# Scores of an attention kernel as 64 by 64 products on four tiles of TensorE's array

## The chip, the cores and the metric

The kernel runs on one core of one Trainium2 chip. The metric is the device time of one execution in microseconds. A core has TensorE (matrix products; its loads of stationary weights are listed apart), VectorE, ScalarE, GpSimd and SyncE, and 16 DMA engines. TensorE holds a stationary operand in an array of 128 rows by 128 columns; a moving operand streams past it, column by column, and the products are summed in PSUM. The array can be addressed in parts: by row halves (an operand with 64 rows), by column halves (64 output rows), or by both.

## The reference, cut to what matters

`reference.py` computes, for 4 batches, 8 heads, 576 positions and head width 64, causal attention mixed with a memory term, and then a two-layer network:

```python
scores = scale * np.matmul(q, k.transpose(0, 1, 3, 2))
scores = np.where(causal, -1000000000.0, scores)
a = np.exp(scores - scores.max(-1, keepdims=True))
a /= a.sum(-1, keepdims=True) + 1e-09
local = np.matmul(a, v)
...
out = g * mem_out + (1 - g) * local
h = x @ w_in
g = np.maximum(h, 0.0) + np.log1p(np.exp(-np.abs(h)))
return g @ w_out
```

The input `x` of the network is `out` with its 8 heads side by side (2304 rows of 512), and the hidden width is 2048. All operands are fp32.

## The kernel before, in words

Heads are taken in pairs: `p` counts 4 pairs, and a pair's two heads of 64 channels fill the 128 partitions of a q or k tile (head 0 in partitions 0 to 63, head 1 in 64 to 127). Each pair of each batch is worked in two windows of query positions: window A holds chunks 0 and 1 (positions 0 to 255), window B holds chunks 2, 3 and 4 (256 to 575, the last chunk with 64 positions). That makes 32 halves (4 batches, 2 windows, 4 pairs).

For each half, in the names of the code: q and k are loaded (`qA`, `kA`, or `qB`, `kB`, L986 to L998); `memory` (L770) makes the memory term (`sm`, then `mA` or `mB`); `chunks` (L503) makes the scores (`s`, a PSUM tile of two banks, one for each head), their row maxima (`nm`, L548), the powers (`P`, L559) and the normalized weights, which are turned either by TensorE (`turned`, L668) or by a transposing DMA (`PTA` or `PTB` from `PHL`, L629); and `values` (L819) sums memory term and weighted values in `xp` (L825, L837, L852). When a block of positions has its four pairs, `fill` (L897) runs the first 7 of the network's 16 hidden blocks on it (L384) beside the attention of the next; `rest` (L920) does the others at the end (L384, L950). Weights are unpacked by `decode` (L466), partly with TensorE products (L488, L489).

The scores are made in `scores` (L521). For chunks 0 to 3 each head is one product call (L528): the stationary operand is 128 query positions of the head's 64 partitions, the moving operand the keys up to and including the chunk (128, 256, 384 or 512 columns), and the output is 128 partitions of the head's bank. An fp32 product call leaves two weight loads and two matmuls in the trace. The two heads lie on the two row halves of the array. Chunks 0 and 1 are made in one go (8 matmul records), chunks 2 and 3 each by itself (4 records). Chunk 4 takes both heads on the full array (L532). After the products of each go, the causal mask is added by products with an identity (L539 for window A, L543 for chunks 2 and 3, L534 for chunk 4), and VectorE waits for the last of these.

The order of every engine's work is fixed ahead by a planner (`Plan`, L95): it takes the operations with estimated durations and ranks (the tables at the head of the file), plays them through, and the instructions are issued in the order that comes out. In stretches where the planner sees TensorE idle it issues spare products (L1033). The scores are one operation of the planner with an estimate of its own (L576).

Of the kernel before, what the change touches and what calls it, by code (L numbers as in the profile page):

```python
# [272 lines left out]
def attn_softplus_moe(  # L273
# [15 lines left out]
    MM = nc.tensor.matmul  # L289
# [213 lines left out]
    def chunks(u, win, b, p, cs, ks):  # L503
# [5 lines left out]
        so = [0, 128] if both else [0] * len(cs)  # L509
# [11 lines left out]
        def scores(js):  # L521
            for j in js:
                c, n, sv, qv, kv = cs[j], ns[j], ss[j](), q()[:, 130:], kk()
                cq = c * 128 - q0
                if c < 4:
                    for h in range(2):
                        rr = slice(64 * h, 64 * h + 64)
                        MM(sv[:, h, so[j]:so[j] + n], lhsT=qv[rr, cq:cq + 128], rhs=kv[rr, :n], start=j == js[0],  # L528
                           stop=True, skip_group_check=True)
                else:  # L530
                    for i in range(2):
                        MM(sv[:, i, :288], lhsT=win.qz(), rhs=kv[:, 288 * i:288 * i + 288], start=True, stop=True)  # L532
            if m == 1:
                MM(sv[:, 1, 224:288], lhsT=identb, rhs=mask4, start=False, stop=True, skip_group_check=True)  # L534
                return
            for h in range(2):
                e = so[js[-1]] + ns[js[-1]]
                if len(js) == 2:
                    MM(sv[:, h, 0:512].rearrange("p (c n) -> p c n", c=2)[:, :, 0:128], lhsT=identb,  # L539
                       rhs=mask.unsqueeze(1).to_broadcast([128, 2, 128]), start=False, stop=True,  # L540
                       skip_group_check=True)
                else:
                    MM(sv[:, h, e - 128:e], lhsT=identb, rhs=mask, start=False, stop=True, skip_group_check=True)  # L543
# [22 lines left out]
        for j, c in enumerate(cs):  # L566
            k, s, nm, pt = ks[j], ss[j], nms[j], pts[j]
            if m == 1:
                win.qz = QZ[win.no // 2 % 2]
                op("POOL", 470, k + RK["qz"], lambda: P.tensor_tensor(  # L570
                    out=win.qz().rearrange("p (h q) -> p h q", h=2),
                    in0=q()[:, 130 + 256:130 + 320].unsqueeze(1).to_broadcast([128, 2, 64]),
                    in1=own.rearrange("p (h q) -> p h q", h=2), op=ALU.mult), r=[q], w=[win.qz])
            if not both or j == 0:
                js = range(len(cs)) if both else [j]
                op("PE", 1080 if both else (450, 660, 968, 1180, 1050)[c], k, lambda js=js: scores(js),  # L576
                   r=[q, kk] + ([win.qz] if m == 1 else []), mode="S" if m == 2 else "f",
                   w=[s] + ([(pt, "s")] if guard else []))
            op("DVE", 147 + 2.08 * ns[j] if m == 2 else 746, k, lambda j=j: maxima(j), r=[s], w=[(nm, j)])
# [23 lines left out]
        for j, c in enumerate(cs):  # L603
            k, pt, phl = ks[j], pts[j], phls[j]
            if c < 4:
                n, nk = ns[j], c + 1
# [367 lines left out]
    for hi_, (b, p, w) in enumerate(halves):  # L974
        u = units[b, p]
        cs, q0, n = WINS[w]
# [114 lines left out]
```

## Time and profile before

| what | us |
|---|---|
| three runs | 612.47, 614.54, 616.35 |
| their median | 614.54 |
| the profiled execution, its own time | 612.59 |
| its span, from the first to the last instruction | 610.8 |

All rows are from that one profiled execution. PE is TensorE's matmuls, PEld its weight loads, DVE is VectorE, ACT ScalarE, POOL GpSimd, SP SyncE; L528 is line 528 of the kernel. A matmul's record runs from its issue to its modelled end, so records that follow one another overlap, and a start may stand ahead of the end of the load that the matmul needs. A shape such as 64*128 is rows by columns of the array; 128*64 has 64 columns.

### The profile page before, as it was taken

To read this page: it belongs to the slowest core of one execution; us is meant where nothing else is said; L and a number is where in the kernel's file an instruction comes from. 1 tells how busy PE (TensorE), PEld (TensorE's weight loads), DVE (VectorE), ACT (ScalarE), POOL (GpSimd) and SP (SyncE) were. 2 spreads that over 40 slices of the span, in tenths; PEclk is the share of its full clock that TensorE was granted. 3 is DMA by queue.
4 is the path that set the end of the run, shared out by engine and by line. 5 is a ranking of instruction groups with operands and counts; after the bars stand their busy time and mean duration, and the time that the engine had idled before them with its cause. 6 is when DMAs were issued, how large, how long until landed. Compare 5 with 4: busy or idle time off the path is not lost.

```text
span 610.8 us, 12312 instructions
## 1 busy us (share of the span) xinstructions
PE 590.8 (97%) x4610; PEld 531.6 (87%) x4610; DVE 353.2 (58%) x805; ACT 302.6 (50%) x854; POOL 170.8 (28%) x262
## 2 busy tenths in 40 slices
PE   6998999999999999999999999999999999999996
PEld 5666769787887787978799999999999999999996
DVE  6778888787877798868982777651212121212121
ACT  5767866566766686668743443433222222222221
POOL 3455433435433434325532344330000000000000
PEclk9999999999999999999999999999999999999999
DMA  8634559958999799966976643333314140522011
GB/s 314 212 131 147 168 161 230 174 202 180 194 198 216 187 179 193 171 172 158 174 124 172 214 136 122 105 126 117 104 36 129 47 135 3 169 72 70 1 44 35
DMA packets 129243, 87.38 MB, mean 143 GB/s; under 512 B 86176, under 2 KB 120992, under 8 KB 129184
## 3 DMA queue, kind: packets, MB, share of 16 engines
q1 hardware_dynamic: 129184, 86.60, 55.4%
q8 instruction: 36, 0.59, 0.4%
q14 instruction: 23, 0.19, 0.1%
HBM read 47.88 MB, written 18.22 MB: 108 GB/s over the span
## 4 chain that ended last, share of the span: by engine, by line
PE 65%; DMA 2%; DVE 1%; SPq 0%; ACT 0%; POOL 0%; issue 0%; DVEq 0%; ACTq 0%
PE h L384 35%; PE s L950 21%; PE s L528 3%; PE xp L837 3%; PE s L532 1%; PE sm L799 1%; DMA PTA<-PHL 1%; PE xp L825 1%; DMA qA<-in_nat_dram 1%; DMA kA<-in_nat_dram 1%; PE s L543 1%; DVE PHL L620 0%; DVE vb L763 0%; PE s L539 0%; SPq L914 0%
## 5 line engine op out<-in xcount | busy, mean ns | idle before, releaser
L384 PE MATMUL h<-xhl,w 128*128 128x256 f32 (+1 forms) x1536 | 227.8, 298 | 0.0
L384 PEld LDWEIGHTS h<-xhl,w 128*128 128x128 f32 x1536 | 210.5, 189 | 1.6 <-issue 0.5
L317 DVE TENSOR_TENSOR g<-gl,g 128x256 fp32r<-128x256 f32 (+1 forms) x128 | 60.0, 472 | 161.9 <-ACT g L323 161.7
L887 ACT ACTIVATE gl<-h 128x256 f32<-128x256 f32 (+1 forms) x128 | 52.1, 409 | 179.3 <-PE h L384 176.9
L950 PE MATMUL s<-g,w 128*128 128x320 f32 (+1 forms) x948 | 139.3, 297 | 0.0
L950 PEld LDWEIGHTS s<-g,w 128*128 128x128 f32 x948 | 131.1, 188 | 0.0
L384 PE MATMUL h<-g,w 128*128 128x256 f32 (+1 forms) x588 | 87.1, 299 | 0.0
L616 POOL TENSOR_SCALAR PHL<-P,rr 128x384 f16<-128x384 f32 (+3 forms) x100 | 57.2, 588 | 80.1 <-DVE rr L596 22.2
L384 PEld LDWEIGHTS h<-g,w 128*128 128x128 f32 x588 | 78.7, 190 | 0.7
L559 ACT ACTIVATE P<-s,nm 128x256 f32<-128x256 f32 (+3 forms) x128 | 66.4, 525 | 5.2 <-DVE PHL L620 2.6
L548 DVE TENSOR_REDUCE nm<-s 128x2 f32<-128x768 f32 (+2 forms) x64 | 51.4, 818 | 12.8 <-PE s L543 7.2
L323 ACT CAST g<-gl 128x256 fp32r<-128x256 f32 (+1 forms) x128 | 55.1, 433 | 3.9
L620 DVE SCALAR_TENSOR_TENSOR PHL<-P,rr,PHL 128x384 f16<-128x384 f32 (+3 forms) x100 | 56.0, 594 | 0.8 <-POOL PHL L616 0.8
L317 POOL TENSOR_TENSOR w<-wu,w 128x512 fp32r<-128x512 f32 x23 | 30.5, 1328 | 28.8 <-ACT w L323 28.8
L353 POOL TENSOR_SCALAR wu<-wu 128x512 f32<-128x512 f32 x32 | 20.4, 641 | 45.0 <-DVE wu L349 40.3
L528 PE MATMUL s<-kB,qB 64*128 64x384 f32 (+1 forms) x128 | 32.7, 588 | 0.0
L837 PEld LDWEIGHTS <-vb 128*64 128x64 f16 x508 | 24.6, 110 | 8.2 <-issue 2.4
L791 POOL TENSOR_TENSOR ph<-ph,pe 128x320 f32<-128x320 f32 (+1 forms) x22 | 18.5, 843 | 31.5 <-ACT pe L783 21.0
L360 DVE SCALAR_TENSOR_TENSOR wu<-ws,wu 128x512 int32<-128x512 int32 x32 | 26.6, 832 | 0.9
L559 ACT ACTIVATION_READ_ACCUMULATOR P<-s,nm 128x1 f32 x128 | 25.5, 199 | 0.0
L323 ACT CAST w<-wu 128x512 fp32r<-128x512 f32 x29 | 17.9, 618 | 13.9 <-DVE wu L364 13.7
L554 ACT ACTIVATE nm<-nm 128x2 f32<-128x2 f32 (+2 forms) x64 | 12.9, 201 | 23.9 <-DVE nm L548 17.3
(123 smaller groups left out, 648.9 us busy)
## 6 DMA issues: line engine op xcount, KB each, us to landing
ws<-in_w_in_dram SPq DMA_DIRECT2D x16, 512.0 KB, 3.7
ws<-in_w_out_dram SPq DMA_DIRECT2D x16, 512.0 KB, 3.4
va<-in_nat_dram SPq DMA_DIRECT2D x16, 320.0 KB, 4.0
xd<-xhl SPq DMA_DIRECT2D x16, 320.0 KB, 3.1
kB<-in_nat_dram SPq DMA_DIRECT2D x16, 288.0 KB, 3.7
xd<-xhl SPq DMA_DIRECT2D x16, 256.0 KB, 3.0
xhl<-xd SPq DMA_DIRECT2D x8, 512.0 KB, 4.7
xhl<-xd SPq DMA_DIRECT2D x6, 640.0 KB, 5.0
```

The source lines that it names most:

```text
L317: eng.tensor_tensor(out=out, in0=in0, in1=in1, op=ALU.subtract)
L323: A.copy(out, in_)
L360: V.scalar_tensor_tensor(out=ti(), in0=si(1), scalar=-0x40000000, in1=ti(), op0=ALU.bitwise_and, op1=ALU.bitwise_or)
L384: MM(out, lhsT=l, rhs=r, start=start and i == 0, stop=stop and i == len(pairs) - 1)
L528: MM(sv[:, h, so[j]:so[j] + n], lhsT=qv[rr, cq:cq + 128], rhs=kv[rr, :n], start=j == js[0], stop=True, skip_group_check=True)
L548: V.tensor_reduce(out=nm()[:, 2 * j * both:2 * j * both + 2], in_=s()[:, :, so[j]:so[j] + n], op=ALU.max, axis=AX.X, negate=True)
L559: A.activation(out=pt()[:, po[j] + h * n:po[j] + h * n + n], in_=s()[:, h, so[j]:so[j] + n], func=AF.Softplus, scale=SCALE, bias=nm()[:, o ...
L616: P.tensor_scalar(out=o[:, :, 0, h, :], in0=src, scalar1=rs, scalar2=0.0, op0=ALU.mult, op1=ALU.add)
L620: V.scalar_tensor_tensor(out=o[:, :, 1, h, :], in0=src, scalar=rs, in1=o[:, :, 0, h, :], op0=ALU.mult, op1=ALU.subtract)
L837: MM(xp()[64 * h:64 * h + 64, lo:n], lhsT=vb()[:, vi, kc, 64 * h:64 * h + 64], rhs=ptw()[:, kc * 4 + t * 2 + h, lo:n], start=False, stop=( ...
L887: op("ACT", 170 + .833 * n, -1, lambda: A.activation(out=gl()[:, :n], in_=hp()[:, :n], func=AF.Softplus, scale=XSC), r=[hp], w=[gl])
L950: MM(bank(dm), lhsT=l, rhs=r, start=f == f0 and q == 0 and (not small or dm % 2 == 0), stop=f == NF - 1 and q == 2, skip_group_check=True)
```

## The change

Each of the calls of L528 becomes two, with 64 query positions each: `e` picks the first or the second 64 of the chunk, as columns of the stationary operand and as partitions of the output. The moving operand is the same for both. The calls for the four combinations of head and `e` follow one another, so a go of one chunk has four calls in place of two. The masks, chunk 4, the planner's operations, durations and ranks are not touched.

```diff
                 if c < 4:
                     for h in range(2):
                         rr = slice(64 * h, 64 * h + 64)
-                        MM(sv[:, h, so[j]:so[j] + n], lhsT=qv[rr, cq:cq + 128], rhs=kv[rr, :n], start=j == js[0],
-                           stop=True, skip_group_check=True)
+                        for e in range(0, 128, 64):
+                            MM(sv[e:e + 64, h, so[j]:so[j] + n], lhsT=qv[rr, cq + e:cq + e + 64], rhs=kv[rr, :n],
+                               start=j == js[0], stop=True, skip_group_check=True)
                 else:
```

## Rows read from the trace of the kernel before

**Rows 1.** The page: busy time of each engine, and the granted clock by slice.

```profile
PE 590.8 (97%) x4610; PEld 531.6 (87%) x4610; DVE 353.2 (58%) x805; ACT 302.6 (50%) x854; POOL 170.8 (28%) x262
...
PEclk9999999999999999999999999999999999999999
```

**Rows 2.** Waits of matmuls on other engines: us in total, times, longest.

```profile
PE sm L1033 <- DVE mA L812: 2.9, 2, 2.5
PE s L528 <- DMA kA<-in_nat_dram: 2.7, 2, 1.5
PE sm L1033 <- DVE mB L812: 2.2, 1, 2.2
...
PE xp L837 <- DMA PTA<-PHL: 1.2, 2, 0.8
```

**Rows 3.** Windows: length, each engine's busy time (count), clock, DMA share, GB/s.

```profile
120.00:201.70 81.70, 78.16 (x656) 65.64 (x655) 66.37 (x167) 54.21 (x171) 32.09 (x51) 1.00 0.93 197
201.70:256.90 55.20, 55.20 (x440) 45.83 (x441) 47.34 (x113) 39.23 (x117) 22.80 (x39) 1.00 0.92 182
...
264.30:310.50 46.20, 46.20 (x362) 37.23 (x364) 39.13 (x91) 35.43 (x108) 23.40 (x34) 1.00 0.74 154
310.50:610.80 300.30, 295.65 (x2266) 293.80 (x2262) 101.47 (x192) 91.05 (x213) 37.16 (x39) 1.00 0.32 98
```

**Rows 4.** Waits of weight loads, lines 543 and 539: us, times, longest.

```profile
PEld L543 <- issue: 20.8, 32, 0.8
PEld L539 <- issue: 5.3, 16, 0.3
```

**Rows 5.** Timeline, three groups of line 528: start, us covered, engine, line, names, shape, count.

```profile
20.07 0.52 PEld L528 LDWEIGHTS s<-kA,qA 64*128 64x128 f32 x8 [0.17 <-issue]
...
28.27 0.19 PEld L528 LDWEIGHTS s<-kB,qB 64*128 64x128 f32 x2 [0.21 <-ACT ph L789]
...
28.70 0.49 PE L528 MATMUL s<-kB,qB 64*128 64x384 f32 x2
...
29.12 0.10 PEld L543 LDWEIGHTS <-identb 128*128 128x128 bf16 x1 [0.54 <-issue]
...
36.50 0.30 PEld L528 LDWEIGHTS s<-kB,qB 64*128 64x128 f32 x4 [0.17 <-issue]
...
37.03 0.59 PE L528 MATMUL s<-kB,qB 64*128 64x512 f32 x2
```

**Rows 6.** Line 528 in window B: shortest, median and longest record in ns.

```profile
L528 PEld LDWEIGHTS s<-kB,qB x128: 182/184/187, 28.3 to 304.4; 64*128 64x128 f32 x128
L528 PE MATMUL s<-kB,qB x128: 482/588/694, 28.3 to 304.9; 64*128 64x384 f32 x64, 64*128 64x512 f32 x64
```

**Rows 7.** Timeline, line 852: column halves at 128 by 64 and 64 by 64.

```profile
37.77 0.20 PEld L852 LDWEIGHTS xp<-PTA,va 128*64 128x64 f32 x4
...
38.04 0.39 PE L852 MATMUL xp<-PTA,va 128*64 128x256 f32 x2
38.26 0.39 PE L852 MATMUL xp<-PTA,va 128*64 128x128 f32 x4
...
89.07 0.20 PEld L852 LDWEIGHTS xp<-PTB,va 64*64 64x64 f32 x4 [0.28 <-issue]
89.33 0.19 PEld L488 LDWEIGHTS h<-wu,ident 128*128 128x128 f32 x1
```

**Rows 8.** Timeline, line 528 where TensorE came out of a wait.

```profile
7.76 0.55 PEld L528 LDWEIGHTS s<-kA,qA 64*128 64x128 f32 x8 [1.72 <-DMA qA<-in_nat_dram]
...
264.27 0.18 PEld L528 LDWEIGHTS s<-kA,qA 64*128 64x128 f32 x1 [1.43 <-DMA qA<-in_nat_dram]
...
264.27 0.22 PEld L528 LDWEIGHTS s<-kA,qA 64*128 64x128 f32 x2 [1.43 <-DMA qA<-in_nat_dram]
```

**Rows 9.** Windows, line 528 alone: length, matmuls (count), loads (count), clock, DMA.

```profile
7.70:201.70 194.00, 28.39 (x164) 11.46 (x164) 1.00 0.76 194
201.70:310.50 108.80, 19.14 (x92) 6.66 (x92) 1.00 0.83 170
```

## The prediction

> **What bounds the kernel now.** I read the page first, then the waits of TensorE, the spans by stretch, and last single groups of line 528 in the timeline. The page shows TensorE's matmuls busy for 97% of the span with the granted clock in the top tenth in all forty slices; no other engine is above 58% [rows 1]. A busy matmul record is no proof that the array streams, since records overlap, so the waits count: all that TensorE waited for another engine or a transfer is a few microseconds, the longest entries 2.9 us for mA, 2.7 us for kA, 2.2 us for mB, and 1.2 us for PTA [rows 2]. By stretch [rows 3], the granted clock is 1.00 throughout (the level of 2.4 GHz), and matmuls cover 55.20 of 55.20 us from 201.7 to 256.9 and 46.20 of 46.20 us from 264.3 to 310.5, and all of the rest after that: there the program's end moves with TensorE's own time, one for one. Before 201.7 the cover is thinner: from 120 on 78.16 of 81.70, with the DMA engines 93% busy. In that part a transfer or VectorE can end a wait that a faster TensorE only makes longer.
>
> **Where line 528 stands.** It runs in 48 groups: 16 of window A (chunks 0 and 1 in one go) and 32 of window B (chunk 2 or chunk 3), counted by the loads of the mask products that close each [rows 4]. One group is read in the timeline [rows 5]. Each product is in fp32 and leaves two records, so two passes. In the chunk 2 group the loads start at 28.27, the second passes at 28.70 and the next line's load at 29.12. The two row halves go side by side: both products' first passes lie between 28.27 and 28.70, and both second passes start within 0.01 us at 28.70 (two records of 482 ns [rows 6] cover 0.49). In a chunk 3 group the loads start at 36.50 and the second passes at 37.03. Going from 384 to 512 columns adds 0.10 or 0.11 us to a pass (28.27 to 28.70 is 0.43, 36.50 to 37.03 is 0.53), so a pass costs 0.107 us per 128 columns: 0.32 for 384, and the first pass has 0.43 - 0.32 = 0.11 us ahead of it. That is the load of 128 weight columns with nothing over it; the second load lies under the first pass. Behind the last pass stands 29.12 - 28.70 - 0.32 = 0.10 us before the next load. A group of window A has four passes in a row on each half, two of 128 columns and two of 256, and eight loads that cover 0.52 us from 20.07.
>
> **What the change does to a group.** The diff replaces each product by two of half the output rows. That is 256 products in place of 128, and twice the records in each group: 256 loads and 256 matmuls more in all. Columns streamed per product stay as they are, and so does the number of passes in a row on each tile, if the four tiles go side by side. Terms per group:
>
> 1. The head. A load of 64 columns is in the trace [rows 7]: in line 852's group the loads start at 37.77, the second passes (256 columns) at 38.04 and the next products at 38.26. A pass is 0.22, so the load ahead of the first is 38.04 - 37.77 - 0.22 = 0.05 us, half of the 0.11 above. Gain 0.053 us, taking 0.107 us for 128 columns and half of it for 64.
>
> 2. The passes. Line 852 also shows two column halves on different weights side by side at 128 by 64, at the same 0.22 us for 256 columns as elsewhere, and its last products show the exact tile of the change, 64 by 64 [rows 7]: loads at 89.07, next engine work at 89.33, 0.26 us for two products of two passes of 64 columns. Side by side that should take 0.05 + 2 x 0.053 + 0.10 = 0.26; one after the other 0.37. So column halves of one row half go side by side, and row halves do so at line 528. All four at once stand in no row. I take them as side by side, cost 0; the other end is that the second pair starts only when the first is through: 0.64 us more in each of the 32 groups of window A and chunk 2, 0.85 us in the 16 of chunk 3, plus a head.
>
> 3. The start of the later tiles. Warm, the second half's load starts under 0.01 us after the first (two loads of some 183 ns cover 0.19) [rows 5, 6]; I take 0.0065 us per tile. Four tiles have three such steps, two have one, so the tail ends 0.013 us later. In four groups TensorE came out of a wait, and the second half started some 0.03 us late: their eight loads cover 0.55 in place of 0.52, as in the first of the four, at 7.76, and of the third, at 264.27, one load covers 0.18 and two 0.22 [rows 8]. Three such steps would cost 0.11 against 0.036 now: 0.072 more, less the head's 0.053, so 0.02 us lost in each of those four.
>
> 4. The drain of 0.10 us on both sides is there before (128 by 128 to row halves and back) and behind 64 by 64 as well (89.07 + 0.05 + 0.11 = 89.23, next load 89.33). Nothing changes. The masks, the maxima and the planner's order stay, so no other engine gets or loses an instruction, and no wait is added: the semaphore that VectorE waits for comes from the mask product.
>
> Sum: 44 x (0.053 - 0.013) - 4 x 0.02 = 1.76 - 0.08 = 1.7 us of TensorE's time. Bounds with the four tiles side by side: 48 x 0.053 = 2.5 us gained if the later tiles cost nothing, 0 or some loss if they all start as in the group of rows 8 (below).
>
> **What reaches the end.** Of line 528's 256 matmul records 164 start before 201.7 and 92 behind [rows 9]. A group of window A leaves eight, one of window B four: 12 and 17 groups before, 4 and 15 behind. Behind 201.7 the 19 groups, two of them of the kind of rows 8, give 17 x 0.04 - 2 x 0.02 = 0.64 us, which I count in full. The 29 before give 27 x 0.04 - 2 x 0.02 = 1.04 us; that passes through waits for kA, PTA and the m tiles [rows 2], some of which hang on earlier products and move with them, and some on transfers in the 93% stretch. Ends: 0 and 1.04; nothing in the rows favours one, so half, 0.52. Total 1.2 us.
>
> The profiled execution took 612.59 us, span 610.8 and 1.8 around it: 611.4 after. It lies low among the runs shown (612.47, 614.54, 616.35), so against the median of 614.54 I predict **613.3 us**, 0.2% less. Within 1%, 6 us, a measurement of this kernel can hardly tell it from no change.
>
> **A rule that speaks against it.** In rows 5 the second product's first pass starts with the first product's first pass, at 28.27, and 0.43 us before that product's second pass at 28.70, although the code issues the first product whole before the second. The Trainium skill ("TensorE: Matmul & The Clock Gate", Part 3, The mechanism) says that matmuls start and end strictly in program order. If a product's two passes stand together in the program, as the code's order suggests, the trace disagrees; by that rule each tile's first pass would wait for the second of the tile before, three passes more in a group of window B (0.96 or 1.28 us) and some 0.85 in one of window A: 16 x (0.96 + 1.28 + 0.85) = 49 us, about 662 us in all. It has 1 of the first rival's 6 in a hundred, since two tiles would already show it.
>
> **Rivals.**
> *The tiles go in pairs (slower).* Place: the third and fourth tile of each group. If something that two tiles fit into (a read path, a place for waiting loads) doesn't take four, the second pair runs after the first. Price by term 2: 32 x 0.64 + 16 x 0.85 + 48 x 0.05 = 36.5 us, less the head's 2.5: 34 us, about 647 us. For it: no row has four. Against: each pair of directions is there at full speed, and a row half already holds products back for its second pass without stopping its neighbour. It decides from 0.053 us of delay on, and shows as over 1% from some 0.18 us of delay per group (6.1 / 48 + 0.053). Chance 6%.
> *Issue sets the start (a little slower).* Twice the records in the same time; if the tiles of all groups start 0.036 us apart as in rows 8, the last starts 0.108 after the first, 0.101 later than now, less 0.053: 48 x 0.048 = 2.3 us more, 616.8 on the median. The point is a step of 0.02 us per tile, (0.053 + 0.0065) / 3. For it: rows 8; against: 44 of 48 groups have their records queued already. Chance 11%.
> *The gain is hidden.* The 1.04 us of the front is waited out, and the gain behind 201.7 is met by a transfer too, since DMA is 92% busy to 256.9: 0 to 0.3 us, 614.3. Chance 15%.
> *The change doesn't do what it says* (the halves of 64 columns load no faster, or run as one): 614.5, counted with the last.
> The forecast has 65%; 3% are left for a gain of more than 1%, for which no row speaks: the whole of line 528's uncovered loads is 2.5 to 5 us.
>
> **How the numbers follow.** Forecast and the two small rivals lie within 1%: 65 + 11 + 15 = 91%, of which I give 1 to noise of the runs; slower by over 1% has the pairs and that noise, 7%; faster 3%. Range: the small cases reach from 614.54 - 2.5 = 612.0 to 616.8. The runs lie 2 us to either side of their median; that much goes below the low end, and the high end, which only the least likely of the small cases reaches, is rounded up: 610.0 to 617.0. The pairs stay out of it.
>
> **What would show it.** Right: at line 528 loads of 64 columns, 512 matmul records; chunk 2's group 0.81 us from the first load to the mask's in place of 0.85 (29.12 - 28.27); four loads starting within 0.02 us; second passes of a chunk 2 group 0.38 us after the first load. Wrong: second passes later than 0.43 us, a chunk 2 group above 0.85 us, or third and fourth tiles that begin where the first pair's second pass does.

## The result, and the profile after

The changed kernel takes 610.74 us (median of 20 executions, 608.48 to 614.14); the kernel before, timed beside it, 616.53 us (20 executions, 611.94 to 619.83). The ratio is 0.9917 with a 95% interval of 0.9895 to 0.994. A second comparison gave 0.9929 (0.9905 to 0.9953). So the change makes the kernel about 0.8% faster, 4 to 5 us by these ratios (in the first comparison the means differ by 5.1 us, the medians by 5.8), where 0.2% was forecast. The measured time lies in the stated range, and the size is four times the forecast's.

The two profiled executions alone would not show this. They differ by 2.0 us: 612.59 before, 610.60 after, spans 610.8 and 608.8 (and the second holds a slow start that its page does not show, told below). The page of the changed kernel, with the lines that answer to [rows 1]:

```profile
span 608.8 us, 12824 instructions
...
PE 590.4 (97%) x4866; PEld 528.5 (87%) x4866; DVE 353.0 (58%) x805; ACT 302.4 (50%) x854; POOL 173.0 (28%) x262
...
PEclk9999999999999999999999999999999999999999
```

TensorE has 256 matmul records and 256 loads more, as counted, and no other engine's count moved. Busy time says nearly nothing of the gain, 590.8 to 590.4 us, since the records of tiles that go side by side cover one another.

The groups of the scores are line 529 now. Their timeline, with the columns of [rows 5], in the order window A, chunk 2, chunk 3:

```profile
21.18 0.43 PEld L529 LDWEIGHTS s<-kA,qA 64*64 64x64 f32 x16 [0.17 <-issue]
22.00 0.11 PEld L540 LDWEIGHTS <-identb 128*128 128x128 bf16 x2 [0.39 <-issue]
...
29.30 0.15 PEld L529 LDWEIGHTS s<-kB,qB 64*64 64x64 f32 x4 [0.21 <-ACT ph L790]
...
29.68 0.50 PE L529 MATMUL s<-kB,qB 64*64 64x384 f32 x4
...
30.11 0.11 PEld L544 LDWEIGHTS <-identb 128*128 128x128 bf16 x2 [0.60 <-issue]
...
37.49 0.21 PEld L529 LDWEIGHTS s<-kB,qB 64*64 64x64 f32 x8 [0.17 <-issue]
...
37.97 0.61 PE L529 MATMUL s<-kB,qB 64*64 64x512 f32 x4
...
38.51 0.11 PEld L544 LDWEIGHTS <-identb 128*128 128x128 bf16 x2 [0.81 <-issue]
```

Read the chunk 2 group. Four loads cover 0.15 us; one takes 0.13 (below), so the last starts 0.02 after the first. All four second passes start around 29.68, 0.38 us after the first load, where [rows 5] had 0.43: four records of 482 ns cover 0.50, so they too lie within 0.02. The mask's load comes at 30.11, 0.81 after the first load, in place of 0.85. The four tiles go side by side. Taken over all 16 groups of each kind, the median from the first load to the mask's falls from 0.846 to 0.806 us (chunk 2), from 1.059 to 1.019 (chunk 3) and from 0.856 to 0.811 (window A).

Line 529 by itself, shortest, median and longest record in ns, answering to [rows 6]:

```profile
L529 PEld LDWEIGHTS s<-kB,qB x256: 129/131/133, 29.3 to 302.5; 64*64 64x64 f32 x128
L529 PE MATMUL s<-kB,qB x256: 482/562/640, 29.3 to 302.9; 64*64 64x384 f32 x64, 64*64 64x512 f32 x64
```

A load's record is 131 ns in place of 184: 0.053 us less, which is the head's term. The shortest matmul record, a second pass of 384 columns, is 482 ns in both kernels.

Groups behind a wait, answering to [rows 8]. First one of the kernel before, from its first load to the mask's:

```profile
179.19 0.55 PEld L528 LDWEIGHTS s<-kA,qA 64*128 64x128 f32 x8 [1.18 <-ACT P L559]
180.07 0.11 PEld L539 LDWEIGHTS <-identb 128*128 128x128 bf16 x2 [0.33 <-issue]
```

then the changed kernel:

```profile
178.28 0.46 PEld L529 LDWEIGHTS s<-kA,qA 64*64 64x64 f32 x16 [1.86 <-ACT P L560]
179.12 0.11 PEld L540 LDWEIGHTS <-identb 128*128 128x128 bf16 x2 [0.39 <-issue]
...
192.75 0.43 PEld L529 LDWEIGHTS s<-kA,qA 64*64 64x64 f32 x16 [1.65 <-DMA qA<-in_nat_dram]
...
266.52 0.13 PEld L529 LDWEIGHTS s<-kA,qA 64*64 64x64 f32 x1 [1.35 <-issue]
...
266.52 0.17 PEld L529 LDWEIGHTS s<-kA,qA 64*64 64x64 f32 x2 [1.35 <-issue]
...
266.52 0.19 PEld L529 LDWEIGHTS s<-kA,qA 64*64 64x64 f32 x5 [1.35 <-issue]
```

At 266.52 the second tile starts 0.04 late, as before, but the third and the fourth follow at the usual step (five loads cover 0.19). The late start is paid once in a group, not once for each tile: 178.28 to 179.12 is 0.84 us, against 0.885 us in the kernel before's groups of this kind (179.19 to 180.07 above). Not every wait brings it: the group at 192.75 has its sixteen loads in 0.43 us, like the warm one at 21.18.

The waits of matmuls on other engines, answering to [rows 2]:

```profile
PE s L529 <- DMA kA<-in_nat_dram: 4.6, 4, 1.7
PE sm L1034 <- DVE mA L813: 2.7, 2, 2.3
...
PE sm L1034 <- DVE mB L813: 0.6, 1, 0.6
...
PE xp L838 <- DMA PTA<-PHL: 0.2, 1, 0.2
```

The wait for mB is 1.6 us shorter than in [rows 2], those for kA are 1.9 longer. These move from execution to execution of one and the same kernel (a second profile of the kernel before had 4.3 for kA), so no single one of them is the gain.

### The profile page after: what moved, and what is told of

It reads as the page before. It is cut to its first block, busy times and chain, and to the rows that moved or that the text cites. A ratio compares the mean times of both kernels' runs of the same rounds, so it can differ in the third digit from the quotient of the medians.

```text
span 608.8 us, 12824 instructions
## 1 busy us (share of the span) xinstructions
PE 590.4 (97%) x4866; PEld 528.5 (87%) x4866; DVE 353.0 (58%) x805; ACT 302.4 (50%) x854; POOL 173.0 (28%) x262
## 4 chain that ended last, share of the span: by engine, by line
PE 86%; DMA 5%; DVE 4%; ACT 1%; SPq 1%; POOL 1%; issue 1%; DVEq 0%; ACTq 0%; POOLq 0%
PE h L384 43%; PE s L951 21%; PE s L529 6%; PE xp L838 4%; PE sm L800 3%; PE s L533 2%; DMA kA<-in_nat_dram 2%; PE xp L853 2%; PE xp L826 1%; PE s L544 1%; PE h L488 1%; DMA qA<-in_nat_dram 1%; PE s L715 1%; DVE nm L549 1%; DMA PTA<-PHL 1%
## 5 line engine op out<-in xcount | busy, mean ns | idle before, releaser
L529 PE MATMUL s<-kB,qB 64*64 64x384 f32 (+1 forms) x256 | 31.4, 561 | 0.0
L678 POOL TENSOR_SCALAR P<-P,rr 128x256 f32<-128x256 f32 (+4 forms) x31 | 18.6, 613 | 20.5 <-DVE rr L597 10.7
```

Source lines behind the costliest of these rows:

```text
L529: MM(sv[e:e + 64, h, so[j]:so[j] + n], lhsT=qv[rr, cq + e:cq + e + 64], rhs=kv[rr, :n], start=j == js[0], stop=True, skip_group_check=True)
```

## The experiments

Each kernel was timed beside the kernel before, and each execution comes with its mean granted clock. With 269 executions (122 of the kernel before) the readings can be set on one footing: a least-squares fit with one level for each kernel and one slope gives 0.48 us (0.42 to 0.53) for each 0.001 by which the granted clock lies under 1.00. The table has the ratio of the comparison, the mean clock and mean time of the kernel's executions, and the fit's level at a clock of 1.00 against that of the kernel before, with its 95% interval.

| kernel | ratio (95%) | mean clock | mean us | at clock 1.00 | against before |
|---|---|---|---|---|---|
| before (122) | | 0.9944 | 614.8 | 612.1 | |
| changed (32) | 0.9917, 0.9929 | 0.9969 | 611.1 | 609.6 | -2.5 ± 0.5 |
| first 16 halves (12) | 0.9958 (0.9933 to 0.9984) | 0.9958 | 613.3 | 611.3 | -0.9 ± 0.8 |
| last 16 halves (12) | 0.9967 (0.994 to 0.9995) | 0.9953 | 613.6 | 611.4 | -0.7 ± 0.8 |
| refill, 96 columns (12) | 0.9979 (0.9955 to 1.0003) | 0.9957 | 613.4 | 611.3 | -0.8 ± 0.8 |
| refill, 288 columns (12) | 1.0009 (0.9984 to 1.0033) | 0.9944 | 615.8 | 613.2 | +1.0 ± 0.8 |
| before with spare products (12) | 0.999 (0.9963 to 1.0018) | 0.9972 | 615.3 | 614.0 | +1.9 ± 0.8 |
| masks on the tiles (19) | 0.991, 0.9926 | 0.9940 | 609.8 | 607.0 | -5.2 ± 0.6 |
| eight tiles (12) | 1.0036 (1.0006 to 1.0065) | 0.9940 | 616.5 | 613.6 | +1.5 ± 0.8 |
| changed, columns cut in two (12) | 1.0053 (1.0029 to 1.0077) | 0.9931 | 617.3 | 613.9 | +1.8 ± 0.8 |
| before, columns cut in two (12) | 1.0009 (0.9983 to 1.0034) | 0.9958 | 614.5 | 612.5 | +0.4 ± 0.8 |

The comparisons with a clock for both kernels ran at four times, on three chips. With a level of the kernel before for each time, the changed kernel (12 executions) is at -2.2, the first and the last 16 halves at -1.2 and -1.0, the changed kernel with columns cut at +2.4 and the kernel before with columns cut at +1.0, each ± 0.8 to 0.9.

### Where the 5 us come from: the two kernels again

The question: the groups hold 2 us and 5 were measured. The kernel before, unchanged:

> The kernel before, unchanged, timed against itself, to see how its executions spread and which granted clock each shows. Theory A (TensorE's own time): the 48 groups give 2.0 us, and the rest of the 5 us measured is executions of the kernel before that spend more time at the lower clock level: then its executions here show granted clocks under 1.00 oftener or lower than those of the changed kernel, and those at 1.00 take some 612 us. Theory B (waits): the front's waits for transfers shrink by more than TensorE saved: then executions of the kernel before at granted clock 1.00 still take 614 us or more.

The changed kernel:

> The changed kernel again, on the same chip as the kernel before. Both theories: 5 us less than the kernel before (0.989 to 0.994). Theory A: executions at granted clock 1.00 some 2 us under those of the kernel before at 1.00. Theory B: at equal granted clock the 5 us stay.

The kernel before against itself: ratio 1.0 (0.9978 to 1.0021). Its 12 executions had granted clocks of 0.993 in the mean, none above 0.995. The changed kernel's 12 had 0.9977. At equal clock the gain is 2.5 us, the rest of the difference in means (614.8 - 611.1 = 3.7) is clock: (0.9969 - 0.9944) x 480 = 1.2 us. The executions of the kernel before lie at 612.1 for clock 1.00, as theory A has it, and not at 614 or more. That also tells what was odd in the profile before: it caught an execution at clock 1.00, and only 20 of the 122 had 0.998 or more, so its 612.59 lay low.

What a low clock is, the profile of this second execution of the kernel before shows: three stretches of 3.4 us around 264 us, each with its length, the engines' busy times and counts, granted clock, DMA share and GB/s:

```profile
260.90:264.30 3.40, 1.10 (x16) 0.86 (x10) 0.31 (x2) 0.34 (x2) 0.00 (x0) 1.00 0.86 197
264.34:267.75 3.41, 3.33 (x17) 2.65 (x18) 2.07 (x5) 2.57 (x7) 0.73 (x1) 0.50 1.01 208
267.76:271.20 3.44, 3.44 (x38) 2.87 (x38) 1.79 (x4) 2.56 (x11) 0.00 (x0) 1.00 0.39 142
```

and TensorE's waits for kA in the same execution (total, times, longest):

```profile
PE s L528 <- DMA kA<-in_nat_dram: 4.3, 2, 2.4
```

TensorE waited 2.4 us for kA; then its clock stood at 0.50, the 1.2 GHz level, for 3.41 us, and 17 matmuls went through where the next stretch of that length has 38 (of other shapes). The group of scores in it took 1.61 us from its first load to the mask's, in place of 0.885:

```profile
264.39 0.96 PEld L528 LDWEIGHTS s<-kA,qA 64*128 64x128 f32 x8 [2.60 <-DMA qA<-in_nat_dram]
266.00 0.13 PEld L539 LDWEIGHTS <-identb 128*128 128x128 bf16 x2 [0.65 <-issue]
```

One such stretch lowers the mean by 3.41 x 0.5 / 612 = 0.0028, which by the fit's slope costs 1.3 us. Not every wait of that length is followed by one: in the profile of the refill with 96 columns (below) TensorE idles for 2.2 us at 190 us and for 2.1 at 261, and its clock stays at 1.00 behind both.

The recorded clock misses something, too. On the changed kernel's page it is 1.00 throughout, yet the first group of scores runs at half the pace. The stretch of that group, in the columns of [rows 3], and its loads:

```profile
7.62:9.14 1.52, 1.49 (x16) 0.76 (x17) 1.14 (x3) 1.17 (x4) 0.56 (x2) 1.00 1.06 402
```

```profile
7.62 0.76 PEld L529 LDWEIGHTS s<-kA,qA 64*64 64x64 f32 x16 [1.57 <-DMA qA<-in_nat_dram]
9.14 0.13 PEld L540 LDWEIGHTS <-identb 128*128 128x128 bf16 x2 [0.76 <-issue]
```

That is 1.52 us, where such a group takes 0.84. The clock's record in this trace begins at 10.98 us, and what lies before counts as 1.00; five of the fourteen profiles show this. So a mean clock can leave out a low stretch at the start, and "at equal clock" means at equal recorded clock.

### Do the front's waits swallow the gain?

```diff
+                        st = 64 if win.no < 16 else 128
-                        for e in range(0, 128, 64):
+                        for e in range(0, 128, st):
```

(with `e + st` for `e + 64`; in the other kernel `win.no >= 16`).

> The change in the first 16 of the 32 halves alone (batches 0 and 1, up to some 165 us), 24 of the 48 groups, 1.0 us of TensorE's time. Theory A (one for one): 1.0 us less than the kernel before at granted clock 1.00, half the changed kernel's gain there. The prediction's account (half of the front is waited out): 0.5 us or less. If the front's waits swallow it: nothing.

> The change in the last 16 halves alone, the other 24 groups, 1.0 us of TensorE's time. Theory A: 1.0 us less at granted clock 1.00. The prediction's account: 0.8 to 1.0 us, more than the early half. If the clock makes the rest of the gain: half of it in each of the two, with the granted clock between that of the two kernels.

Against the kernel before at equal clock -0.9 and -0.7, each ± 0.8; the ratios are 0.9958 and 0.9967. The front half gives no less than the back half, and both together 1.6 ± 1.1, which agrees with the changed kernel's 2.5. The prediction's halving of the front isn't borne out, but the intervals don't tell 1.0 from 0.5 in one half by itself. The profiles answer the question from the other side: the gaps in which TensorE has neither a matmul nor a load, added up from its first record to its last, come to 13.4 and 12.5 us in the two profiles of the kernel before and to 11.7 and 12.9 in the two of the changed kernel. So the waits did not grow by what the groups shrank. The granted clocks lie between those of the two kernels.

### Giving the 0.04 us back

The tile of zeros, `nul`, is made and cleared ahead; the product that uses it:

```diff
...
                 else:
                     MM(sv[:, h, e - 128:e], lhsT=identb, rhs=mask, start=False, stop=True, skip_group_check=True)
+                if h == 0:
+                    MM(sv[:, h, 0:96], lhsT=identb, rhs=nul, start=False, stop=True, skip_group_check=True)
```

> The changed kernel with one more product per group, an identity with 96 columns of zeros added to the scores behind the first mask: it changes no sum, and gives TensorE back the 0.04 us that the four tiles save in each group. Theory A with the end moving one for one: the time of the kernel before, within 1 us at equal granted clock. If the four tiles do more than save that time (a clock that falls less often, say), it stays some 3 us faster than the kernel before. Theory B: as the kernel before too.

A chunk 2 group with the masks, from its first load to the next line's, takes 0.921 us here, 0.878 in the changed kernel and 0.918 before (28.24 to 29.16 in the timeline of this kernel):

```profile
28.24 0.21 PEld L531 LDWEIGHTS s<-kB,qB 64*64 64x64 f32 x8
...
29.16 0.20 PEld L830 LDWEIGHTS xp<-ident,mA 128*128 128x128 f32 x2
```

Of the changed kernel's gain at equal clock 1.7 of 2.5 us is gone again, for 48 x 0.043 = 2.1 us put back: one for one within the interval. So the four tiles bring what they save in TensorE's time, and little that is left when that is taken back. With three times the columns:

> The refill with 288 columns in place of 96: 0.12 us more in each of 48 groups than the changed kernel, 5.9 us. One for one: 615.5 us at granted clock 1.00 where the changed kernel takes 609.6, and the kernel before 612.0. A dose that moves the end by more than itself (9 us, half as much again as the 96 columns seemed to give) would take 618 or more; one that is partly hidden in waits, under 614.

For 48 x 0.123 = 5.9 us put in, the end moved by 613.2 - 609.6 = 3.6 us. A larger dose is partly taken up in the waits, whose gaps come to 9.7 us in this kernel's profile; nothing is amplified.

### Is it the waits that let the clock fall?

```diff
         def scores(js):
+            if both and win.no in (18, 19, 26):
+                last = [h.t for h in R["sm"].opened if h.t is not None][-1]
+                for _ in range(5):
+                    MM(last[:, 390:512], lhsT=ident, rhs=ident[:, 0:122], start=True, stop=True)
             for j in js:
```

> The kernel before with five spare products of TensorE (1.1 us) ahead of the scores in three halves of window A where it waited for a load (at 179, 193 and 264 us). If the low clock comes behind such waits and costs its part of the kernel before's time: granted clock up from 0.994 to 0.996 or more, and 0.5 to 1.5 us less than the kernel before. If the clock has nothing to do with these waits: same clock, and up to 1 us more where the products are not hidden.

The clock rose from 0.9944 to 0.9972, as the first alternative said, and the time did not fall: 615.3 against 614.8 in the mean. The products cost 1.9 us at equal clock, of 3 x 1.1 = 3.3 put in, and the clock gave 0.0028 x 480 = 1.3 us back. This speaks for some of the low stretches of the kernel before hanging on TensorE standing idle in these waits; an edit that leaves these waits alone, the columns cut in the kernel before, moved the mean clock by half as much (0.9958). Why the changed kernel has fewer of them isn't shown: its profile has idle time at the same three places.

### The masks on the scores' tiles

The mask is added by the same four tiles (a copy of each 64 rows of the mask lies in both row halves), so that the array's parts are switched once less in a group. The lines for chunks 2 and 3 (window A's change likewise):

```diff
...
-                    MM(sv[:, h, e - 128:e], lhsT=identb, rhs=mask, start=False, stop=True, skip_group_check=True)
+                for g in range(2):
+                    d = slice(64 * g, 64 * g + 64)
+                    MM(sv[d, h, e - 128:e], lhsT=identb[rr, rr], rhs=mk[rr, g, :], start=False, stop=True,
+                       skip_group_check=True)
...
```

> The changed kernel with the masks of chunks 0 to 3 also as products of 64 by 64, each on its scores' tile, so that the array isn't switched between scores and mask. If the 0.09 us between the last score pass and the mask's load is the switch of the array's parts, it goes in 48 groups: 4 us of TensorE's time less than the changed kernel. Theory A: the end moves by about that, 606 to 607 us where the changed kernel takes 610.7. Theory B: more than that where waits follow, under 605. If the gap is the matmuls' own drain, nothing changes.

> The changed kernel with the masks on the scores' tiles once more, since it had seven timed runs only. If it beats both kernels: 0.988 to 0.994 of the kernel before, its runs at granted clock 1.00 at 606 to 607.5 us where the changed kernel takes 609.6. If the first reading was luck: 609 us or more there.

The timeline of a chunk 2 group of this kernel, its loads, the masks' loads, and the first load of the next line:

```profile
63.52 0.21 PEld L533 LDWEIGHTS s<-kB,qB 64*64 64x64 f32 x8 [0.56 <-ACT PTB L732]
63.89 0.13 PEld L551 LDWEIGHTS <-identb 64*64 64x64 bf16 x4 [0.17 <-issue]
64.38 0.20 PEld L834 LDWEIGHTS xp<-ident,mB 128*128 128x128 f32 x2 [0.36 <-issue]
```

and the same group of the changed kernel:

```profile
64.48 0.21 PEld L529 LDWEIGHTS s<-kB,qB 64*64 64x64 f32 x8 [0.56 <-ACT PTB L724]
65.28 0.11 PEld L544 LDWEIGHTS <-identb 128*128 128x128 bf16 x2 [0.60 <-issue]
65.36 0.20 PEld L826 LDWEIGHTS xp<-ident,mB 128*128 128x128 f32 x2
```

The masks' loads now go under the score passes (0.37 us after the first load, in place of 0.80), and the last mask product starts 0.72 us after the first load in place of 0.88. But the gap of about 0.1 us has only moved: it stands behind the masks now, and the next line's load comes 0.86 after the first load in place of 0.88. So the 0.09 us goes with the switch of the array's parts, since the masks don't pay it any more, and a group gets rid of it only where another group with the same tiles follows: there a chunk 2 group takes 0.70 us to the next group's first load, in place of 1.02. From each group's first load to the next line's or group's, the 48 groups add up to 3.4 us less in the second profile of this kernel than in the first of the changed one. The end gained 2.6 ± 0.7 us at equal clock (607.0 against 609.6), of the 4 expected. Against the kernel before the ratios are 0.991 (0.9877 to 0.9943) and 0.9926 (0.9896 to 0.9957). It beats the kernel before, and the changed kernel by the fit. By the plain medians (609.84 and 609.35 against 610.74 and 610.52) the lead over the changed kernel is small, because its clock was lower, 0.9940.

### Cutting further

```diff
-                        for e in range(0, 128, 64):
+                        for e in range(0, 128, 32):
```

(with `e + 32`).

> The scores cut once more, into products of 64 by 32 on eight tiles. By the two terms of the prediction the head falls by another 0.027 us and four more tiles start 0.0065 us apart: 0.027 - 0.026 = nothing gained, chunk 2's group stays at 0.81 us and the time at the changed kernel's, 609 to 610.5 us at granted clock 1.00. If eight don't go side by side, chunk 2's group doubles to some 1.5 us and the time goes up by 30 us or more.

The timeline of the chunk 2 group: eight tiles' loads, their second passes, and the mask's load.

```profile
29.61 0.18 PEld L529 LDWEIGHTS s<-kB,qB 64*32 64x32 f32 x16 [0.21 <-ACT ph L790]
...
29.96 0.53 PE L529 MATMUL s<-kB,qB 64*32 64x384 f32 x8
...
30.41 0.11 PEld L544 LDWEIGHTS <-identb 128*128 128x128 bf16 x2 [0.62 <-issue]
```

The group is what the two terms gave: second passes 0.35 after the first load, eight records of 482 ns that cover 0.53, and 0.80 to the mask's load (median 0.806 over the 16, as with four tiles). Eight tiles go side by side. Yet the kernel is slower than the kernel before, 1.0036, and 4.0 us slower than the changed one at equal clock. The group doesn't hold that loss. Two kernels look for it in the number of records:

```diff
-                            MM(sv[e:e + 64, h, so[j]:so[j] + n], lhsT=qv[rr, cq + e:cq + e + 64], rhs=kv[rr, :n],
-                               start=j == js[0], stop=True, skip_group_check=True)
+                            for x in (0, n // 2):
+                                MM(sv[e:e + 64, h, so[j] + x:so[j] + x + n // 2], lhsT=qv[rr, cq + e:cq + e + 64],
+                                   rhs=kv[rr, x:x + n // 2], start=j == js[0] and not x, stop=True,
+                                   skip_group_check=True)
```

> The changed kernel with the moving operand of each score product cut in two: as many records as with eight tiles (1024 matmuls at the scores' line), tiles of 64 by 64 and the columns streamed as in the changed kernel. If the number of records is what made eight tiles 4 us slower at equal granted clock: 613 to 615 us at granted clock 1.00 though the groups take as long as in the changed kernel. If it is the tile of 32 columns: 609.5 to 610.5 us there.

> The kernel before with the moving operand cut in two wherever it has over 128 columns: 448 matmuls at the scores' line where the changed kernel has 512, tiles and columns as before. If records cost by themselves, the kernel before gets 1 to 2 us slower at equal granted clock (613 to 614), and the changed kernel's gain is what is left after such a loss. If not: 612 to 612.5 us, the kernel before.

With 1024 matmuls at the scores' line and tiles of 64 by 64, the level is 613.9, 4.3 us above the changed kernel; so a loss of that size needs no tile of 32 columns. But this kernel's groups are longer: its tiles start 0.0135 us apart, twice the usual step, and chunk 2 takes 0.831, chunk 3 1.044, window A 0.892 us to the mask's load, 16 x (0.025 + 0.025 + 0.081) = 2.1 us in all. That leaves some 2 us outside the groups, beside 4 us with eight tiles, so the tile of 32 columns may still have a part in those 4. With 448 matmuls in the kernel before the groups grow by as much (16 x (0.012 + 0.012 + 0.113) = 2.2 us) and the end moves by 0.4 ± 0.8 (1.0 ± 0.9 against the kernel before of the same time). So at 448 matmuls records outside the groups cost nothing that can be seen, and at 1024 the kernels lose 2 and 4 us outside them. By the profiles it is lost in waits: the gaps of TensorE come to 16.1 us with eight tiles and 14.8 with the columns cut, against 11.7 and 12.9 in the changed kernel (10.1 in the kernel before with columns cut). The profiles show matmuls waiting longest for the same thing, first in the kernel with eight tiles, then in that with the columns cut in two:

```profile
PE s L529 <- DMA kA<-in_nat_dram: 4.9, 4, 1.5
...
PE s L529 <- DMA qA<-in_nat_dram: 2.8, 1, 2.8
```

```profile
PE s L530 <- DMA kA<-in_nat_dram: 4.0, 2, 2.2
PE s L530 <- DMA qA<-in_nat_dram: 3.2, 1, 3.2
```

That is 7.7 and 7.2 us of waits for the loads of window A, where the changed kernel's two profiles have 4.6 + 1.5 and 4.3 + 1.6. Whether records delay these loads, and how, is open.

## Why the prediction was right or wrong

**The head: right.** 0.053 us forecast; the loads' records fell by 0.053, and the second passes of chunk 2 come at 0.38 in place of 0.43. The rows of another line that used 64 columns carried it.

**The passes: right.** Four tiles at once stood in no row, and each pair of directions did. They go side by side at full speed, and so do eight. The rival with pairs, 647 us, is out, and so are the 662 us of the strict order: four tiles' first passes start within 0.02 us here, although each product has a second pass 0.38 us later. The Trainium skill ("TensorE: Matmul & The Clock Gate", Part 3, Measured speedup vs the span model) has each further tile of a packed array add about 4 ns of issue. The trace has 6 to 7 ns from tile to tile. Whether the strict order itself, which the Trainium skill states on the same page (Part 3, The mechanism), is broken stays open: that hangs on the order in which a product's two passes are issued, and no run shows it.

**The start of later tiles: right warm, wrong for a late start.** Warm, 0.02 us for the fourth tile, as taken. In four groups the prediction charged the late start of 0.036 us three times and expected 0.02 us lost in each. It is paid once: such a group of window A takes 0.84 us where it took 0.885, 0.045 gained. The rival in which issue sets the start fell with that. That the four groups came out of a wait was a misreading, which changes no term. In the kernel before the group at 193.51 came out of one and started at the usual step, and the last of the four, at 268.14, started late with no wait ahead of it:

```profile
193.51 0.52 PEld L528 LDWEIGHTS s<-kA,qA 64*128 64x128 f32 x8 [1.46 <-DMA qA<-in_nat_dram]
```

```profile
268.14 0.55 PEld L528 LDWEIGHTS s<-kA,qA 64*128 64x128 f32 x8
```

What makes a group start late is open.

**The sum in the groups: 1.7 us forecast, 16 x (0.040 + 0.040 + 0.045) = 2.0 measured.** Of the 0.3, 4 x 0.065 = 0.26 lie in the four groups that start late, and the rest in the other groups of window A, which gained 0.045 in place of 0.040.

**What reaches the end: wrong, as far as the intervals tell.** The step that failed is "The 29 before give [...] Ends: 0 and 1.04; nothing in the rows favours one, so half, 0.52". Half of the front's share would leave 1.4 of the groups' 2.0 us; the whole change gave 2.5 ± 0.5 at equal clock, the two kernels with half the change 0.9 and 0.7 with no less from the front, and TensorE's gaps did not grow in the profiles. The fit's 2.5 against the 2.0 of the groups is on the edge of its interval; whether 0.5 us come from shorter waits is open. The rival in which the gain is hidden is out. A reading beside this one is wrong at no cost: in [rows 3] matmuls cover 295.65 of the 300.30 us behind 310.5, not all, but the 4.6 us that are missing stand behind the last product, in both kernels.

**What was left out: the clock.** The prediction took the granted clock as 1.00, as the one profile showed, and compared two executions at that level. In 122 executions of the kernel before it is 0.9944 in the mean, and 0.9969 in 32 of the changed kernel. This is worth 1.2 us of the 3.7 between the means. In the comparison that gave 5 us the kernel before had a median of 616.5, 1.7 us above its median over those 122 (614.8), so part of the 5 is chance. That the clock differs is measured; that it differs because of the four tiles isn't shown. The half changes and the refill lie between the two, but the kernel with the masks on the tiles has four tiles and a clock of 0.9940, and the kernel before with columns cut has none and 0.9958.

**The range: held by its margin.** No case within 1% that the prediction priced lies under 612.0 us. The 610.74 measured falls in the range because of the 2 us set aside for the spread of the runs, and that is luck as far as the mechanism goes.

## What to carry to other kernels

A product that fills only part of the array's rows can be cut along its columns as well: the first weight load, which nothing covers, is halved, the passes cost nothing more as long as the tiles go side by side, and each further tile costs one start step of 0.0065 us, so that a group gains nothing beyond four tiles here. Look for the price in lines that already use such a tile; with head, pass, step and drain read from a few groups, the sum for a warm group came out to a few ns.

Where one profile is all there is, ask at which granted clock it was taken, where the clock's record begins, and how often executions reach that clock. A wait of 2.4 us on the bounding engine can cost more than 1 us again in low clock behind it, and an engine that runs without a gap only behind its last wait may pass on savings from ahead of it as well.

## What the runs showed of the hardware that was not expected

- Behind a wait of 2.4 us TensorE ran at the lower clock level for 3.41 us, though it had work all through. Over executions of one kernel the time goes by 0.48 us for each 0.001 of mean granted clock, which holds about half of the variance (0.56 in the 122 of the kernel before, 0.50 in the 32 of the changed one).
- The page's granted clock can be 1.00 over a stretch at half speed: the clock's record began at 10.98 us, and a group of scores at 7.62 took 1.52 us in place of 0.84.
- A late start of the second tile (0.036 us) is paid once by a group of four tiles. It came behind some waits and not behind others.
- Eight tiles of 64 by 32 go side by side too: eight second passes of 482 ns within 0.53 us.
- The start step belongs to the product call: two calls on a tile before the next tile's, and the tiles start 0.0135 us apart in place of 0.0065.
- The switch of the array's parts, some 0.1 us, was paid at each change of tile shape that was read, and moved when a neighbouring line took the same tiles.
- Twice as many products at the scores' line made the kernel 4 us slower at equal clock, of which the groups hold 0 (eight tiles) or 2.1 us (columns cut); the rest is waits of TensorE, and what lengthens them is open.
